# One slot size for the rest of an attention and mixture-of-experts kernel

## The chip, the cores and the metric

The kernel runs on one core of a Trainium2 chip. The metric is the device time of one execution in microseconds (us), the median over runs. The engines are named PE (TensorE), DVE (VectorE), ACT (ScalarE), POOL (GpSimd) and SP (SyncE); PEld is PE's weight load.

## What is computed

First an attention over 8 batches of 8 heads, 576 tokens of 64 values each, that keeps only the scores within `tau` of the row's maximum; then each of the 4608 tokens (512 values) goes through the one of 8 experts that its gate picks:

```python
scores = scale * np.matmul(q, k.transpose(0, 1, 3, 2))
thresh = np.max(scores, axis=-1, keepdims=True) - tau
scores = np.where(scores >= thresh, scores, -1000000000.0)
attn = softmax(scores)
x = concat_heads(np.matmul(attn, v))                  # 4608 x 512
logits = x @ w_gate + modality_bias[modality_id]
e_idx = np.argmax(logits, axis=1)
for e in range(8):
    mask = e_idx == e
    h = np.maximum(x[mask] @ w1[e], 0.0)              # 512 -> 1024
    out[mask] = gate_w[mask, None] * (h @ w2[e])      # 1024 -> 512
```

## The kernel before, in words

The attention goes through 32 pairs of heads, 9 steps to a pair. When a batch is done, its tokens are routed: `route_a` to `route_b` give every token a place, and `scatter` (line 681) writes its number and its gate's weight into a table `tab` in DRAM with indirect DMAs of POOL. The table has one region of CAP rows for each expert, and a row that holds no token holds the number N, which later gathers and scatters skip. The table is filled with N early on, in `late_constants` (lines 256 to 259): POOL sets a tile `fill`, and SP writes it out. `fill` shares the tag `xr` with the tiles in which the attention's output leaves.

While the attention runs, full slots of tokens are already sent through their expert, interleaved with it: SIDE (line 71) lists seven of them, of 256, 384, 512, 512, 512, 448 and 512 rows. `pick` (line 691) chooses the expert for each. What is left at the end, the rest, is planned by `pick_rest` (line 708) on DVE, on one partition: for three slot sizes, 512, 384 and 256 (SIZES), it counts how many slots each expert needs, and gives the expert and the table position of each slot, in `si`. ALWAYS slots of 512 rows (three) are written into the program without a condition; all others lie in a nest of branches at the end (`more`, line 1202), within an outer branch on the number of further slots (lines 1209 to 1214), which each engine loads by `ask` (line 1125). Before the outer branch ACT copies one value of the last output tile into `done_y` (line 1210).

`slot` (line 780) writes one slot. SP loads the expert and the table position into registers (lines 795 and 799), then the table rows `tb` (line 801) and the weights `raw` (lines 838 and 842). POOL gathers the tokens, 128 rows to a tile `xg` (line 814). PE transposes them (line 828); weights and tokens are each split into a high and a low part (lines 303, 304, 856 to 860), and each product takes three matmuls. The first layer is line 874, its ReLU lines 885 and 886. The second layer, line 901, goes over 2 halves of the hidden layer, the row tiles, and 4 chunks in each; ACT (line 909) and DVE (line 914) scale and add the halves, and POOL scatters the tile `y` to the output (line 916).

PE's and POOL's orders are those in which the code is written out, by due times (`at`, `put`); the orders of DVE, ACT and SP are the framework's scheduler's, within chains that `stamp_issue_order_token` fixes. `finish` (line 1112) gives the attention's memory back and opens new pools for the rest, their buffers and the planning's tiles among them; from there the matmuls write into new PSUM banks, `pm`, in place of `bk`.

## Time and profile before

| | |
|---|---|
| runs | 1012.5, 1012.56, 1022.66 us |
| median | 1012.56 us |
| the profiled execution's own time | 1011.88 us |
| its span, first to last instruction | 1010.2 us |
| granted TensorE clock, mean | 0.998 |

The profile is of one execution. A busy time is that of an engine's instructions, without its waits; PE's matmuls overlap, and their ends are modelled. A wait is put down to what ended it. A `q` behind an engine's name is its sequencer, which branches, loads registers and issues DMAs. In the chain of waits, "issue" is time for which the profile shows no wait.

### The profile page before, as it was taken

The numbers are of one execution on the slowest core, as the hardware profiler recorded it, in microseconds if no ns is written. First come the engines' busy times: TensorE is split into PE (matmuls) and PEld (weight loads), VectorE is DVE, ScalarE is ACT, GpSimd is POOL, SyncE is SP. The second block draws the span as 40 slices with busy tenths as digits, with TensorE's granted clock in tenths as the row PEclk, the third lists the DMA queues.
The fourth block names the chain that finished last, engine by engine and source line by source line (L and its number), as shares of the span: only waits on it lengthen the run. The fifth ranks groups of instructions, "written<-read, shape, count | busy, mean of one in ns | idle before, by whom it ended". The sixth has DMA issues, their size and how long they took to land.

```text
span 1010.2 us, 20293 instructions
## 1 busy us (share of the span) xinstructions
PE 986.6 (98%) x6556; PEld 795.0 (79%) x6556; DVE 681.3 (67%) x1698; ACT 633.5 (63%) x1439; POOL 524.8 (52%) x728
## 2 busy tenths in 40 slices
PE   7999999999999999999999999999999999999996
PEld 6777777788888887788778888788878867888885
DVE  6888987778677766777677877777766764333422
ACT  6787887676676666666667666666667625334430
POOL 4363467377538553655455654646567274534311
PEclk9999999999999999999999999999999999999999
DMA  6667777679647665676647555667666227634301
GB/s 154 145 158 169 137 196 196 169 161 237 170 124 168 187 159 133 144 184 163 165 112 177 153 158 133 152 160 197 153 150 165 82 81 200 204 108 139 116 10 44
DMA packets 206803, 151.83 MB, mean 150 GB/s; under 512 B 100062, under 2 KB 167646, under 8 KB 206688
## 3 DMA queue, kind: packets, MB, share of 16 engines
q1 hardware_dynamic: 199488, 131.53, 53.0%
q0 software_dynamic: 7200, 18.92, 5.9%
q8 instruction: 54, 0.88, 0.4%
q14 instruction: 61, 0.50, 0.2%
HBM read 80.05 MB, written 19.48 MB: 99 GB/s over the span
## 4 chain that ended last, share of the span: by engine, by line
PE 74%; DVE 9%; issue 9%; DMA 2%; ACT 2%; POOL 2%; SPq 1%; POOLq 0%; DVEq 0%; ACTq 0%
PE bk L521 15%; PE s L402 14%; PE bk L487 10%; PE bk L901 10%; PE bk L874 10%; PE pm L901 4%; PE pm L874 3%; DVE pr L459 2%; DVE nm L435 2%; PE bk L339 2%; PE bk L828 2%; PE bk L512 1%; PE bk L573 1%; ACT e L445 1%; DMA xg<-xs,tb 1%
## 5 line engine op out<-in xcount | busy, mean ns | idle before, releaser
L435 DVE TENSOR_REDUCE nm<-s 128x1 f32<-128x576 f32 x254 | 190.9, 752 | 97.4 <-PE s L402 95.3
L459 DVE SCALAR_TENSOR_TENSOR pr<-s,nm,e 128x576 f32<-128x576 f32 x254 | 204.8, 815 | 62.7 <-ACT e L445 58.9
L445 ACT ACTIVATE e<-s,nm 128x576 f32<-128x576 f32 x254 | 188.6, 743 | 59.5 <-DVE nm L435 52.6
L402 PE MATMUL s<-km,q 128*128 128x288 f32 x1024 | 196.5, 313 | 7.5 <-DVE pr L459 6.4
L497 ACT COPY ptm<-bk 128x512 f32<-128x512 f32 x256 | 149.4, 584 | 53.2 <-PE bk L487 52.6
L487 PE MATMUL bk<-ident,pr 128*128 128x128 f32 x1152 | 173.8, 273 | 0.0
L402 PEld LDWEIGHTS s<-km,q 128*128 128x128 f32 x1024 | 146.3, 189 | 24.5 <-DVE pr L459 18.2
L487 PEld LDWEIGHTS bk<-ident,pr 128*128 128x128 f32 x1152 | 140.6, 140 | 27.3 <-issue 6.2
L521 PE MATMUL bk<-ptm,v_m 128*64 128x320 f32 (+1 forms) x1024 | 140.7, 412 | 0.3 <-DVE hl L886 0.3
L860 POOL TENSOR_TENSOR w2l<-raw,w2h 128x512 fp32r<-128x512 f32 x77 | 98.5, 1287 | 32.6 <-ACT w2h L856 28.6
L521 PEld LDWEIGHTS bk<-ptm,v_m 128*64 128x64 f32 x1024 | 68.2, 136 | 50.8 <-issue 7.9
L916 POOL DMA_INDIRECT out_dram<-y,tb x37 | 38.0, 1026 | 122.2 <-DVE y L914 92.2
L476 ACT COPY rp<-pr 128x64 f32<-128x64 f32 x271 | 60.0, 248 | 43.8 <-DVE pr L459 41.5
L874 PE MATMUL bk<-xh,w1h 128*128 128x512 f32 (+3 forms) x204 | 82.1, 402 | 0.1
L313 POOL CAST nk<-str 128x64 fp32r<-128x64 f32 x31 | 7.4, 240 | 138.3 <-ACT str L327 130.9
L874 PE MATMUL bk<-xl,w1h 128*128 128x512 f32 (+3 forms) x204 | 74.2, 363 | 0.0
L874 PE MATMUL bk<-xh,w1l 128*128 128x512 f32 (+3 forms) x204 | 74.1, 363 | 0.0
L901 PE MATMUL bk<-w2h,hh 128*128 128x512 f32 x168 | 73.4, 437 | 0.0
L860 POOL TENSOR_TENSOR w1l<-raw,w1h 128x512 fp32r<-128x512 f32 x53 | 68.1, 1285 | 4.2
L901 PE MATMUL bk<-w2h,hl 128*128 128x512 f32 x168 | 66.2, 394 | 0.0
L901 PE MATMUL bk<-w2l,hh 128*128 128x512 f32 x168 | 66.1, 393 | 0.0
L814 POOL DMA_INDIRECT xg<-xs,tb x37 | 39.0, 1053 | 38.4 <-DMA tb<-tab 16.5
(211 smaller groups left out, 1973.6 us busy)
## 6 DMA issues: line engine op xcount, KB each, us to landing
raw<-in_moe_w_dram SPq DMA_DIRECT2D x160, 256.0 KB, 3.5
q<-nq SPq DMA_DIRECT2D x124, 256.0 KB, 4.4
km<-nk SPq DMA_DIRECT2D x124, 144.0 KB, 2.5
v_m<-in_v_dram SPq DMA_DIRECT2D x32, 256.0 KB, 3.7
xs<-xr SPq DMA_DIRECT2D x32, 256.0 KB, 3.0
k_m<-in_k_dram SPq DMA_DIRECT2D x62, 128.0 KB, 3.2
q_m<-in_q_dram SPq DMA_DIRECT2D x62, 128.0 KB, 3.7
vr<-in_v_dram SPq DMA_DIRECT2D x64, 16.0 KB, 4.1
```

The lines of the kernel that those rows point to most:

```text
L402: nc.tensor.matmul(out=sps[:, hf, 0:SH], lhsT=a, rhs=x, start=(z == 0), stop=(z == len(passes) - 1))
L435: in_line(nc.vector.tensor_reduce(out=nm[:, 0:1], in_=sv, axis=AX.XY, op=ALU.max, negate=True), two)
L445: in_line(nc.scalar.activation(out=e, in_=sv, func=AF.Exp, bias=nm[:, 0:1]), two and n < LEAD)
L459: in_line(nc.vector.scalar_tensor_tensor(out=pr.rearrange("p (a x) -> p a x", a=2), in0=s2[n % 2][:, :, 0:SH], scalar=th, in1=e, op0=ALU.i ...
L476: (nc.gpsimd.tensor_copy if 2 <= n < 46 else nc.scalar.copy)(out=state[("rp", p)][:, 2 * c + s + x, :], in_=pr[:, SA:S])
L487: nc.tensor.transpose(out=ps[:, kc * P:(kc + 1) * P], in_=pr[:, kc * P:(kc + 1) * P], identity=ident)
L497: in_line(nc.scalar.copy(out=ptm[:, s, :, (c % 2) * P:(c % 2 + 1) * P], in_=pv), n + 2 < LEAD)
L521: nc.tensor.matmul(out=o, lhsT=lhsT, rhs=rhs, start=start, stop=stop, skip_group_check=True)
L814: nc.gpsimd.indirect_dma_start(out=xg, out_offset=None, in_=xs[0:nrow, :], in_offset=bass.IndirectOffsetOnAxis(ap=box["tb"][:, t, 0:1].bit ...
L860: then(eng.tensor_tensor(out=lo, in0=raw, in1=hi.bitcast(F32), op=ALU.subtract), eng is nc.vector and (lined or late))
L874: nc.tensor.matmul(out=ps[:, 0:WT], lhsT=a[:, cs], rhs=x[:, c, :], start=(c == 0 and z == 0), stop=(c == KC - 1 and z == 2))
L901: nc.tensor.matmul(out=ps, lhsT=h[:, ts], rhs=w, start=(z == 0 and y == 0), stop=(z == F2 - 1 and y == 2))
```

## The change

The rest is planned in slots of 512 rows alone. `pick_rest` has one count per expert in place of three and writes a smaller `si`; MAXC, the most slots that can come, becomes 16. The table's regions are one slot longer (CAP from 4608 to 5120 rows), and the table's fill goes out in two DMAs from a tile of half the size. The gathers, the scaling and the scatters work on the rows of their tile that the slot has (`w = TP(t)`), where they worked on 128. At the end, the nest of branches hangs directly on the number of slots, `done_y` and the outer branch go, and so does the packing of two halves (`pack`), which only slots of 256 rows used.

```diff
@@ -61,21 +61,17 @@
     NT = NC + 1
     SH = S // 2
     W = 512
-    CAP = -(-N // W) * W
-    NCH = CAP // W
+    NCH = -(-N // W)
+    CAP = (NCH + 1) * W
     TROWS = NE * CAP + 2 * W
-    WH = W // 2
     WM = 384
     U = 64
-    SIDE = [(WH, 1), (WM, 2)] + [(W if b != B - 2 else W - U, b) for b in range(3, B)]
-    SIZES = (W, WM, WH)
-    MAXN = ((N - NE * (WM + 1)) // W + NE if N >= NE * (WM + 1) else N // (WM + 1),
-            min(NE, N // (WH + 1)), NE)
-    left_ = max(W, N - sum(w for w, _ in SIDE))
-    ALWAYS = (-(-left_ // W), 0, 0)
-    MAXC = max(MAXN)
+    SIDE = [(W // 2, 1), (WM, 2)] + [(W if b != B - 2 else W - U, b) for b in range(3, B)]
+    WR = W
+    MAXC = (N - NE) // WR + NE
+    ALWAYS = -(-max(W, N - sum(w for w, _ in SIDE)) // W)
     KC = DM // P
     FC = DF // P
     scale = 1.0 / float(D) ** 0.5
...
@@ -186,14 +182,12 @@
     lg = glob.tile([P, NT, H + 1, NE], F32, name="lg")
     nc.gpsimd.memset(lg[:, NC], 0.0)
     taken0 = iota([1, NE], [[CAP // U, NE]], "taken0", base=W // U)
-    th_lo = iota([1, NE, NCH], [[0, NE], [W, NCH]], "th_lo")
+    th_lo = iota([1, NE, NCH], [[0, NE], [WR, NCH]], "th_lo")
     ij = iota([1, MAXC], [[1, MAXC]], "ij")
     tri = glob.tile([1, NE, NE], F32, name="tri")
     nc.gpsimd.memset(tri, 1.0)
     nc.gpsimd.affine_select(out=tri, in_=tri, compare_op=ALU.is_ge, fill=0.0,
                             base=0, pattern=[[1, NE], [-1, NE]], channel_multiplier=0)
-    cnt = glob.tile([1, 4, NE], F32, name="cnt")
-    nc.gpsimd.memset(cnt[:, 0], 0.0)
     pay = glob.tile([P, B, NT, 2], I32, name="pay")
     nc.gpsimd.iota(pay[:, :, 0:NC, 0], pattern=[[S, B], [1, NC]], base=0, channel_multiplier=NC)
     nc.gpsimd.iota(pay[:, :, NC, 0], pattern=[[S, B]], base=SA, channel_multiplier=1)
...
@@ -253,10 +247,12 @@
                                         in1=mid_f[:, m, :].unsqueeze(2).to_broadcast(shp), op=ALU.mult)
             nc.gpsimd.tensor_tensor(out=bias_t, in0=bias_t, in1=bias_u, op=ALU.add)
-        fill = work.tile([P, TROWS // P, 2], I32, name="fill", tag="xr", bufs=2)
+        half = TROWS // P // 2
+        fill = work.tile([P, half, 2], I32, name="fill", tag="xr", bufs=2)
         nc.gpsimd.memset(fill[:, :, 0], N)
         nc.gpsimd.memset(fill[:, :, 1], 0)
-        nc.sync.dma_start(out=tab.rearrange("(p r) c -> p r c", p=P), in_=fill)
+        for y in range(2):
+            nc.sync.dma_start(out=tab[y * half * P:(y + 1) * half * P, :].rearrange("(p r) c -> p r c", p=P), in_=fill)
         return bias
...
@@ -714,60 +710,39 @@
         taken = fin["xp"].tile([1, NE], F32, name="taken", bufs=1)
         nc.vector.tensor_tensor(out=taken, in0=done, in1=taken0, op=ALU.subtract)
-        th = fin["xp"].tile([1, 3, NE, NCH], F32, name="th", bufs=1)
-        for z, w in enumerate((WM, WH, 0)):
-            nc.vector.scalar_tensor_tensor(out=th[:, z], in0=th_lo, scalar=float(w),
-                                           in1=left.unsqueeze(2).to_broadcast([1, NE, NCH]),
-                                           op0=ALU.add, op1=ALU.is_lt)
-        nc.vector.tensor_reduce(out=cnt[:, 1:4, :], in_=th, axis=AX.X, op=ALU.add)
...
+        th = fin["xp"].tile([1, NE, NCH], F32, name="th", bufs=1)
+        nc.vector.tensor_tensor(out=th, in0=th_lo, in1=left.unsqueeze(2).to_broadcast([1, NE, NCH]), op=ALU.is_lt)
+        ns = fin["xp"].tile([1, NE], F32, name="ns", bufs=1)
+        nc.vector.tensor_reduce(out=ns, in_=th, axis=AX.X, op=ALU.add)
+        cum = fin["xp"].tile([1, NE], F32, name="cum", bufs=1)
+        t = fin["xp"].tile([1, NE, NE], F32, name="cum_t", bufs=1)
+        nc.vector.tensor_tensor(out=t, in0=ns.unsqueeze(1).to_broadcast([1, NE, NE]), in1=tri, op=ALU.mult)
+        nc.vector.tensor_reduce(out=cum, in_=t, axis=AX.X, op=ALU.add)
         SHP = [1, MAXC, NE]
...
+        le = fin["xp"].tile(SHP, F32, name="le", bufs=1)
+        nc.vector.tensor_tensor(out=le, in0=ij.unsqueeze(2).to_broadcast(SHP),
+                                in1=cum.unsqueeze(1).to_broadcast(SHP), op=ALU.is_ge)
+        ej = fin["xp"].tile([1, MAXC], F32, name="ej", bufs=1)
         nc.vector.tensor_reduce(out=ej, in_=le, axis=AX.X, op=ALU.add)
...
+        si = glob.tile([1, 2 * MAXC + 1], I32, name="si")
+        nc.vector.tensor_scalar(out=si[:, 0:MAXC], in0=ej, scalar1=float(NE - 1), scalar2=None, op0=ALU.min)
+        off = fin["xp"].tile([1, NE], F32, name="off", bufs=1)
+        nc.vector.tensor_tensor(out=off, in0=cum, in1=ns, op=ALU.subtract)
+        nc.vector.tensor_scalar(out=off, in0=off, scalar1=float(-WR), scalar2=None, op0=ALU.mult)
+        nc.vector.scalar_tensor_tensor(out=off, in0=taken, scalar=float(U), in1=off, op0=ALU.mult, op1=ALU.add)
+        em = fin["xp"].tile([1, MAXC], F32, name="em", bufs=1)
         nc.vector.tensor_scalar(out=em, in0=ej, scalar1=float(-NE), scalar2=None, op0=ALU.add)
...
+        nc.vector.tensor_tensor(out=le, in0=em.unsqueeze(2).to_broadcast(SHP),
+                                in1=iota_m[0:1, :].unsqueeze(1).to_broadcast(SHP), op=ALU.is_equal)
+        nc.vector.tensor_tensor(out=le, in0=le, in1=off.unsqueeze(1).to_broadcast(SHP), op=ALU.mult)
+        bj = fin["xp"].tile([1, MAXC], F32, name="bj", bufs=1)
         nc.vector.tensor_reduce(out=bj, in_=le, axis=AX.X, op=ALU.add)
...
+        nc.vector.scalar_tensor_tensor(out=bj, in0=ij, scalar=float(WR), in1=bj, op0=ALU.mult, op1=ALU.add)
         nc.vector.scalar_tensor_tensor(out=bj, in0=ej, scalar=float(CAP), in1=bj, op0=ALU.mult, op1=ALU.add)
...
+        nc.vector.tensor_scalar(out=si[:, MAXC:2 * MAXC], in0=bj, scalar1=float(W), scalar2=float(W + NE * CAP),
+                                op0=ALU.add, op1=ALU.min)
+        nc.vector.tensor_copy(out=si[:, 2 * MAXC:], in_=cum[:, NE - 1:NE])
         return si
     prev_out = []
...
@@ -811,9 +786,10 @@
                 xg = xt_pool().tile([P, DM], F32, name="xg", bufs=nx[1])
                 box[("xg", t)] = xg
+                w = TP(t)
                 nc.gpsimd.indirect_dma_start(
-                    out=xg, out_offset=None, in_=xs[0:nrow, :],
-                    in_offset=bass.IndirectOffsetOnAxis(ap=box["tb"][:, t, 0:1].bitcast(U32), axis=0),
+                    out=xg[0:w], out_offset=None, in_=xs[0:nrow, :],
+                    in_offset=bass.IndirectOffsetOnAxis(ap=box["tb"][0:w, t, 0:1].bitcast(U32), axis=0),
                     bounds_check=nrow - 1, oob_is_err=False)
             return f
...
@@ -904,18 +878,18 @@
                     return
                 let_go(ps)
                 tb = box["tb"]
+                w = TP(t)
                 if g == 0:
                     y0 = xp.tile([P, DM], F32, name="y0", bufs=W // P)
-                    nc.scalar.activation(out=y0, in_=ps, func=AF.Copy, scale=tb[:, t, 1:2].bitcast(F32))
+                    nc.scalar.activation(out=y0[0:w], in_=ps[0:w], func=AF.Copy, scale=tb[0:w, t, 1:2].bitcast(F32))
                     box[("y0", t)] = y0
                     return
                 y = xp.tile([P, DM], F32, name="y", bufs=2)
-                fin["y"] = y
-                nc.vector.scalar_tensor_tensor(out=y, in0=ps, scalar=tb[:, t, 1:2].bitcast(F32),
-                                               in1=box.pop(("y0", t)), op0=ALU.mult, op1=ALU.add)
+                nc.vector.scalar_tensor_tensor(out=y[0:w], in0=ps[0:w], scalar=tb[0:w, t, 1:2].bitcast(F32),
+                                               in1=box.pop(("y0", t))[0:w], op0=ALU.mult, op1=ALU.add)
                 i = _inst(nc.gpsimd.indirect_dma_start(
-                    out=out, out_offset=bass.IndirectOffsetOnAxis(ap=tb[:, t, 0:1].bitcast(U32), axis=0),
-                    in_=y, in_offset=None, bounds_check=N - 1, oob_is_err=False))
+                    out=out, out_offset=bass.IndirectOffsetOnAxis(ap=tb[0:w, t, 0:1].bitcast(U32), axis=0),
+                    in_=y[0:w], in_offset=None, bounds_check=N - 1, oob_is_err=False))
                 for o in prev_out:
                     tc.declare_no_dep(i, o, reason="every token has a row of its own")
                 prev_out.append(i)
...
@@ -1093,14 +1066,14 @@
                 t = when(e[0]) - e[2] - (1.5 if e[3] in late and e[3][0] == 1 else 0)
             at(t, e[1])
-    def last_slot(j, z):
+    def last_slot(j):
         def where():
             si = fin["si"]
-            return si[0:1, z, j:j + 1], si[0:1, z, MAXC + j:MAXC + j + 1]
-        return slot(where, lambda: group_bank(), N, SIZES[z], lambda: fin["wp"], (8, 4, FC),
+            return si[0:1, j:j + 1], si[0:1, MAXC + j:MAXC + j + 1]
+        return slot(where, lambda: group_bank(), N, WR, lambda: fin["wp"], (8, 4, FC),
                     lambda which, f_: nc.vector if which == 1 else nc.gpsimd, (lambda: fin["xp"], (2, 4)),
-                    lined=z + j == 0, pack=2 * SIZES[z] == W)
+                    lined=j == 0)
     fin = {}
...
@@ -1123,17 +1096,17 @@
     at(XF, finish)
     def ask():
-        fin["more"] = nc.values_load(fin["more_i"][0:1, 0:1], min_val=0, max_val=sum(MAXN))
+        fin["more"] = nc.values_load(fin["si"][0:1, 2 * MAXC:], min_val=0, max_val=MAXC)
     at(F0 + C['ask'], ask)
     t0 = F0
-    for z in range(3):
-        for j in range(ALWAYS[z]):
-            for e in sum(last_slot(j, z), []):
-                t = t0 + e[0] if len(e) == 2 else min(t0 + e[0], F0 + e[2])
-                if z + j == 0 and getattr(e[1], "key", 0) in C['first']:
-                    t = F0 - 8.15 + C['first'].index(e[1].key) / 1000
-                at(t, e[1])
-            t0 += SIZES[z] / 16
+    for j in range(ALWAYS):
+        for e in sum(last_slot(j), []):
+            t = t0 + e[0] if len(e) == 2 else min(t0 + e[0], F0 + e[2])
+            if j == 0 and getattr(e[1], "key", 0) in C['first']:
+                t = F0 - 8.15 + C['first'].index(e[1].key) / 1000
+            at(t, e[1])
+        t0 += W / 16
     def run_events(lo, hi):
         while True:
             ts = [x for x in events if lo <= x < hi]
...
@@ -1199,19 +1172,14 @@
         at(NSTEP + LAG + z / 2, f)
     run_events(0, 10 ** 9)
-    def more(cnt, j, z):
-        if j < MAXN[z]:
+    def more(cnt, j):
+        if j < MAXC:
             with tc.If(cnt > j):
-                for e in sorted(sum(last_slot(j, z), []), key=lambda x: x[0]):
+                for e in sorted(sum(last_slot(j), []), key=lambda x: x[0]):
                     e[1]()
-                more(cnt, j + 1, z)
-    done_y = tiny.tile([1, 1], F32, name="done_y", bufs=1)
-    nc.scalar.copy(out=done_y, in_=fin["y"][0:1, 0:1])
-    with tc.If(fin["more"] > 0):
-        for z in range(3):
-            m = nc.values_load(fin["si"][0:1, z, 2 * MAXC:], min_val=0, max_val=MAXN[z])
-            more(m, ALWAYS[z], z)
+                more(cnt, j + 1)
+    more(fin["more"], ALWAYS)
 # ---- launch: one core; inputs and outputs as the reference has them ----
```

## Rows read from the trace of the kernel before

**Rows 1.** The page's first part: busy us (share), instructions of each engine.

```profile
PE 986.6 (98%) x6556; PEld 795.0 (79%) x6556; DVE 681.3 (67%) x1698; ACT 633.5 (63%) x1439; POOL 524.8 (52%) x728
```

**Rows 2.** PE's waits: waited for, us in total, times, longest.

```profile
PE s L402 <- DVE pr L459: 6.4, 11, 1.5
```

**Rows 3.** Table by stage: stretch, us, busy of each engine, clock, DMA share, GB/s.

```profile
825.00:836.00 11.00, 11.00 (x50) 9.12 (x49) 10.07 (x46) 3.52 (x6) 7.46 (x7) 1.00 0.19 45
...
861.00:1002.00 141.00, 140.87 (x631) 114.94 (x629) 44.67 (x66) 48.47 (x83) 47.00 (x42) 1.00 0.33 103
1002.00:1011.00 9.00, 0.00 (x0) 0.00 (x0) 0.75 (x1) 0.19 (x1) 0.98 (x1) 0.70 0.15 55
```

**Rows 4.** Line 901: count, ns min/median/max, first and last start us, shape.

```profile
L901 PE MATMUL bk<-w2h,hh x168: 387/474/500, 173.9 to 811.3; 128*128 128x512 f32 x168
...
L901 PE MATMUL pm<-w2h,hh x128: 389/392/481, 830.6 to 1001.1; 128*128 128x512 f32 x128
```

**Rows 5.** Lines 1211 and 1213, the closing branch, in the same columns.

```profile
L1211 POOLq EVENT_SEMAPHORE  x6: 17/30/43, 1007.7 to 1008.1; - x6
...
L1211 POOLq COMPARE_BRANCH  x1: 53/53/53, 1005.1 to 1005.1; - x1
...
nothing on L1213; most used: ['L521', 'L402', 'L487', 'L874', 'L901', 'L459', 'L445', 'L339', 'L476', 'L512', 'L828', 'L838', 'L842', 'L435', 'L497', 'L573', 'L609', 'L442', 'L860', 'L313', 'L354', 'L119', 'L348', 'L314', 'L858']
```

**Rows 6.** Timeline of DVE, the planning's first and last: start, us.

```profile
825.20 0.15 DVE L712 SCALAR_TENSOR_TENSOR left<-done,pos 1x8 f32<-1x8 f32 x1
...
835.03 0.17 DVE L758 TENSOR_SCALAR si<-bj 1x30 int32<-1x30 f32 x1
```

**Rows 7.** Waits of SP's queue, 815 to 850 us: total, times, longest.

```profile
SPq L842 <- POOL w1l L860: 9.1, 1, 9.1
...
SPq L1126 <- DVE si L758: 0.2, 1, 0.2
```

**Rows 8.** Chain of waits, 836 to 862 us: start, us, what.

```profile
842.74 0.28 SPq L799
...
843.56 3.81 DMA tb<-tab
...
848.17 4.78 DMA xg<-xs,tb
852.96 0.14 issue
853.09 0.63 PE bk L828 x4
```

**Rows 9.** Lines 257 and 259, the table's fill, in the columns of rows 4.

```profile
L257 POOL MEMSET fill<- x1: 384/384/384, 53.5 to 53.5; 128x296 int32 x1
...
L259 SPq DMA_DIRECT2D tab<-fill x1: 537/537/537, 56.0 to 56.0; - x1
```

**Rows 10.** Line 916, and POOL's timeline from 816 us (idle time in brackets).

```profile
L916 POOL DMA_INDIRECT out_dram<-y,tb x37: 971/1017/1395, 233.5 to 1004.7; - x37
...
816.40 1.01 POOL L916 DMA_INDIRECT out_dram<-y,tb  x1 [0.15 <-issue]
...
825.20 0.63 POOL L858 CAST w1h<-raw 128x512 fp32r<-128x512 f32 x1 [2.12 <-PE bk L874]
```

**Rows 11.** Timeline of the tail, without PE, in the columns of rows 6.

```profile
999.26 0.75 DVE L914 SCALAR_TENSOR_TENSOR y<-pm,tb,y 128x512 f32<-128x512 f32 x1 [2.00 <-PE pm L901]
...
1000.28 0.97 POOL L916 DMA_INDIRECT out_dram<-y,tb  x1 [1.77 <-DVE y L914]
...
1002.19 0.75 DVE L914 SCALAR_TENSOR_TENSOR y<-pm,tb,y 128x512 f32<-128x512 f32 x1 [2.18 <-PEq L1211]
1002.98 0.19 ACT L1210 COPY done_y<-y 1x1 f32<-1x1 f32 x1 [11.36 <-DVE y L914]
1004.69 0.98 POOL L916 DMA_INDIRECT out_dram<-y,tb  x1 [3.44 <-issue]
```

**Rows 12.** Groups of POOL's instructions, 0 to 16 us: busy, mean ns, idle before.

```profile
L313 POOL CAST nk<-str 128x64 fp32r<-128x64 f32 x1 | 0.2, 236 | 6.3 <-ACT str L327 6.3
```

More of the change, by code (lines that the diff above doesn't have):

```diff
@@ L724, in pick_rest @@
-        ns = fin["xp"].tile([1, 3, NE], F32, name="ns", bufs=1)
-        nc.vector.tensor_tensor(out=ns, in0=cnt[:, 1:4, :], in1=cnt[:, 0:3, :], op=ALU.subtract)
-        off = fin["xp"].tile([1, 3, NE], F32, name="off", bufs=1)
-        nc.vector.scalar_tensor_tensor(out=off, in0=taken.unsqueeze(1).to_broadcast([1, 3, NE]),
-                                       scalar=float(U) / W, in1=cnt[:, 0:3, :], op0=ALU.mult, op1=ALU.add)
-        cum = fin["xp"].tile([1, 3, NE], F32, name="cum", bufs=1)
@@ L758, in pick_rest @@
-        nc.vector.tensor_scalar(out=si[:, :, MAXC:2 * MAXC], in0=bj, scalar1=float(W + NE * CAP), scalar2=None,
-                                op0=ALU.min)
-        nc.vector.tensor_copy(out=si[:, :, 2 * MAXC:], in_=cum[:, :, NE - 1:NE])
-        more_f = fin["xp"].tile([1, 3, 1], F32, name="more_f", bufs=1)
-        for z in range(3):
-            nc.vector.tensor_scalar(out=more_f[:, z], in0=cum[:, z, NE - 1:NE], scalar1=float(-ALWAYS[z]), scalar2=0.0,
-                                    op0=ALU.add, op1=ALU.max)
```

36 lines of the change are left out of this document (3 added, 33 removed).

## The prediction

> **What bounds the kernel now.** I read the page's busy shares first: TensorE (PE) is busy 986.6 us of a span of 1010.2 us, the next engine, VectorE (DVE), 681.3 us [rows 1]. So what the change can give is what PE stands idle, and what it can take is a new wait of PE. The table by stage then says where the idle time lies: from 861 to 1002 us, while the rest is worked off, PE is busy 140.87 of 141 us, and after 1002 us it has nothing left to do, while the core still runs for 8.2 us more (1010.2 - 1002) [rows 3]. Before 1002 us PE is idle 1002 - 986.6 = 15.4 us in all. The largest entry of PE's waits is 6.4 us in 11 waits for the masked softmax, spread over the attention [rows 2]; the change does not touch that code. The two ends to look at are therefore the planning of the rest (825 to 853 us) and the tail (after 1002 us).
>
> **How often the rest's slot runs.** This decides whether the change moves 46 us or nothing, so it comes first. The second product's line, 901, has 168 groups of three matmuls into the old banks and 128 into the new ones [rows 4]. A slot of 512 rows has 2 halves x 4 row tiles x 4 chunks = 32 such groups; the side slots of 256 and 384 rows have 16 and 24. 168 = 16 + 24 + 4 x 32, and 128 = 32 (the last side slot) + 96: three slots of 512 rows for the rest, which is ALWAYS[0]. Line 1213, the first line inside the closing branch, left no instruction [rows 5], so the kernel's count of further slots was 0: no slot of 384 or 256 rows, at most three of 512. The new count per expert is the number of thresholds 0, 512, 1024, ... below what is left; the old three counts add up to exactly that. So the new plan also comes to at most three slots, and three always run. The reference's own routing says the same: 476, 497 and 499 rows are left with three experts. The matmuls do not change, and neither does a row of the work of these slots, whose last tiles are full tiles.
>
> **The change, part by part.**
>
> *Planning on DVE.* Lines 712 to 769 run 39 instructions between 825.20 us and 835.03 + 0.17 = 835.20 us, 10.0 us with other DVE work between them [rows 6]. The new text has 20. At the 10.0 / 39 = 0.26 us that an instruction now has of the stretch, 19 fewer are worth 4.9 us of DVE. DVE is full in that stretch (10.07 of 11 us), but PE is too (11.00 of 11 us) [rows 3]: it works on the last side slot, which covers the planning. Who is next in line is SyncE (SP), which loads the plan into registers and issues the rest's loads. SP stood there for 9.1 us waiting for a weight buffer that GpSimd (POOL) releases, and only 0.2 us for the plan's last write [rows 7]. So of 4.9 us at most 0.2 us reach SP. From there the chain is exposed: the register load of the table position at 842.74 us, the table rows, the gather of 4.78 us, and the first transpose at 853.09 us, which PE waited for [rows 8]. I take -0.2 us; 0 if POOL still ends last.
>
> *Tail of the plan.* The copy `done_y` on ScalarE (ACT) goes, and the outer branch goes; the count is compared directly. The branch stays one taken branch over code that isn't run (13 nested slots in place of 23). On POOL, the last engine, the branch is at 1005.1 us and the next instruction at 1007.7 us [rows 5]: 2.6 us, before and after. ACT's copy starts at 1002.98 us, when DVE's last output is ready, and POOL's last scatter, which doesn't read it, starts at 1004.69 us [rows 11]: 0 us, covered by POOL's longer path; if the copy had any part in that scatter's delay, see the rivals.
>
> *Set-up.* A memset of POOL goes and one iota grows from 10 to 16 elements. POOL is idle for 6.3 us before its first cast, waiting for ACT [rows 12]: 0 us. Without that cover it would be some 0.1 us.
>
> *Table fill.* The regions grow from 4608 to 5120 rows, the table from 8 x 4608 + 1024 = 37888 to 41984 rows, 328 per partition; the fill is cut into two DMAs of 164. The two memsets on POOL shrink from 384 ns to 384 x 164 / 296 = 213 ns. SP issues one more DMA, 537 ns [rows 9]. Behind it on SP stand the query copies and the next pair's loads, needed steps later; I take 0 us, and 0.5 us if that cover is gone. The Trainium skill (DMA: Bandwidth & Descriptors, Latency and other measured facts) speaks against this part: it gives each such DMA a first-byte cost of about 0.6 us whatever its size. By it, and were the second DMA exposed, the sum would be 0.6 us larger as an estimate; the row shows only the 537 ns of issue.
>
> *Half-filled last tile.* Only the side slot of 448 rows has one. One gather and one scatter move 64 rows in place of 128, and one ACT and one DVE instruction work on 64 partitions. No row shows an indirect DMA of 64 rows; those of 128 take 1017 ns on POOL [rows 10]. Bounds: 0 us saved, if the time does not hang on the rows, up to 0.5 us each, if it halves. The scatter is the one at 816.40 us; a POOL that is earlier there waits longer at 825.20 us, where it waited for PE [rows 10]. So 0 us.
>
> *Memory.* The planning tiles shrink, so the rest's buffers lie elsewhere in the memory that the attention gives back. No row shows which old tile then lies beneath them. From below 0 us; from above one more DMA round before the rest's first tile, for which the nearest row is the table load, 843.56 to 847.37 us, just ahead of the gather [rows 8]: 3.8 us. I take 0, because the attention's stages are over by then.
>
> Sum: -0.2 us. The profiled execution has a span of 1010.2 us and lasted 1011.88 us, 0.68 us under the median of 1012.56 us. I predict 1012.3 us for the median.
>
> **Rivals.**
>
> *The tail loses its gap.* The scatter before the last starts 0.27 us after DVE ends its tile (999.26 + 0.75 = 1000.01, 1000.28); the last one 1.75 us after (1002.94, 1004.69) [rows 11]. In that time ACT copies `done_y` and the engines load the count. If these are what held POOL, 1.5 us go: 1010.8 us. Against it: POOL waits for none of them.
>
> *The rest starts late* (the other side). One of the rest's first buffers now waits for an old tile. It decides from the first 0.1 us, since PE already waits at 853.09 us: up to 3.8 us as above, 1016.1 us. For it: the memory does move. Against it: most of it has been free for long.
>
> *A second taken branch.* The Trainium skill (Runtime: NRT & Kernel Launch, Instruction fetch mechanics) says that a taken branch out of the fetched pages stalls for a fetch; the trace agrees, by the 2.6 us above. If the nest of 13 left each engine by two branches and not one, that would be 2.6 us: 1014.9 us. The code shows one comparison on the path.
>
> *The order drawn up anew.* The instructions of DVE, ACT and SP are laid out by the framework's scheduler, and one more DMA at 56 us can shift what follows. The price is a wait of PE like the 11 for the softmax, 0.58 us each [rows 2]; 18 more of them give 10 us, 1022.8 us.
>
> *A fourth slot.* 192 matmuls and 16 transposes at 140.87 / 631 = 0.22 us [rows 3]: 46 us, 1058 us. It needs a count that differs from the old one, which the counts above exclude but for an error in the new text.
>
> **How the numbers follow.** Forecast 0.65; tail without gap 0.10; rest late 0.12; second branch 0.03; new order, slower 0.06, faster 0.02; fourth slot 0.02. A measurement of this kernel can tell about 1% from no change, 10 us. Within it lie the first four, 0.90; slower by more: 0.06 + 0.02 = 0.08; faster by more: 0.02, since PE's whole idle time before 1002 us is 15.4 us. The range takes in the tail without gap, less the 0.5 us of each half tile's DMA (1010.8 - 1.0 = 1009.8), and the late rest with the exposed DMA issue (1016.1 + 0.5 = 1016.6): 1009.8 to 1016.6 us.
>
> **What would show it.** Right: 128 groups of line 901 in the new banks, DVE's planning down to 20 instructions and near 5 us, PE idle again for about 0.5 us before the first gathered tile, PE busy 986 to 987 us, and some 8 us after PE's last matmul. Wrong: more matmuls, PE waiting longer than 1 us at the first transposes of the rest, new waits of the score matmuls after 56 us, or a last scatter that follows its tile by 0.3 us.

## The result, and the profile after

The changed kernel takes 1029.07 us (median of 7 runs, 1028.34 to 1034.03). The kernel before, run beside it on the same chip, takes 1015.88 us (7 runs, 1012.5 to 1022.66). The ratio is 1.0135, 95% interval 1.0115 to 1.0155: the change makes the kernel slower by 1.35%, where 1012.3 us against 1012.56 was forecast with a range that ended at 1016.6 us. The runs of before that the prediction started from had a median of 1012.56 us; 1.0135 times that is 1026.2 us.

The profiled execution of the changed kernel lasted 1034.03 us, with a span of 1032.3 us (1010.2 before). The page's first part, with the busy time, share and instructions of each engine, answers to [rows 1]:

```profile
PE 993.8 (96%) x6556; PEld 798.7 (77%) x6556; DVE 676.7 (66%) x1679; ACT 633.6 (61%) x1438; POOL 523.1 (51%) x727
```

PE runs the same 6556 matmuls. The table by stage (stretch, us, busy of each engine, clock, DMA share, GB/s) answers to [rows 3]:

```profile
825.00:836.00 11.00, 9.66 (x58) 7.43 (x58) 8.00 (x30) 2.35 (x6) 8.06 (x12) 1.00 0.37 112
...
861.00:1002.00 141.00, 139.31 (x621) 113.43 (x622) 46.22 (x68) 51.00 (x88) 52.94 (x46) 0.99 0.38 113
1002.00:1014.00 12.00, 12.00 (x52) 9.43 (x51) 2.95 (x4) 0.60 (x1) 2.92 (x3) 1.00 0.14 51
1014.00:1032.00 18.00, 0.04 (x1) 0.00 (x0) 0.75 (x1) 0.00 (x0) 0.97 (x1) 0.57 0.08 27
```

PE ends at 1014.0 us in place of 1002.0, and then the core runs for 18 us with nearly nothing busy, where it ran for 8.2. So the 22.1 us of span fall into two parts: 12 us ahead of PE's end, 10 us behind it.

**Behind PE's end.** What fills the tail is not counted as busy: two instructions of POOL's sequencer, INC_SWDGE_SEM (by its name a semaphore update) and DRAIN. They are seen when one asks for the instructions of POOL on the line of the closing branch and on the program's last line, those of the engine's sequencer included (count, ns min/median/max, first and last start). Of before:

```profile
L1211 POOLq INC_SWDGE_SEM  x1: 348/348/348, 1008.2 to 1008.2; - x1
...
L1241 POOLq DRAIN  x3: 40/107/732, 1008.6 to 1009.9; - x3
```

Of after:

```profile
L1177 POOLq INC_SWDGE_SEM  x1: 2468/2468/2468, 1019.2 to 1019.2; - x1
...
L1209 POOLq DRAIN  x3: 40/107/9389, 1021.7 to 1031.6; - x3
```

The first drain of the three grows from 0.73 to 9.39 us, the semaphore instruction ahead of it from 0.35 to 2.47 us: 8.66 + 2.12 = 10.8 us. In the timeline of after, the last scatter (start, us, operation, idle before and its releaser) starts at

```profile
1015.62 0.97 POOL L890 DMA_INDIRECT out_dram<-y,tb  x1 [2.32 <-DVE y L888]
```

that is 0.28 us after DVE ends its tile, where it stood 1.75 us off before [rows 11]. So the tail gains 1.5 us there and loses 10.8, 9.3 us in sum. The 0.7 us that are left of the 10.0 lie in small differences; 0.3 of them are between PE's end and DVE's last tile.

**Ahead of PE's end.** PE's waits (total, times, longest) answer to [rows 2]; the softmax is as before, the gathered rows are not:

```profile
PE s L398 <- DVE pr L455: 6.4, 11, 1.5
PE bk L804 <- DMA xg<-xs,tb: 5.9, 4, 2.1
```

Two of these four waits are near 2 us, at the first tile of the first side slot and at the first tile of the rest, and behind each the clock drops (columns as in the table by stage):

```profile
143.00:147.00 4.00, 3.81 (x17) 2.00 (x17) 1.62 (x7) 0.60 (x2) 1.47 (x2) 0.50 1.00 219
147.00:151.00 4.00, 4.00 (x27) 4.00 (x26) 1.11 (x2) 2.87 (x8) 2.94 (x6) 0.70 0.02 4
...
857.00:862.00 5.00, 3.45 (x16) 2.52 (x14) 2.24 (x5) 4.30 (x8) 3.03 (x3) 1.00 0.83 213
862.00:867.00 5.00, 4.42 (x17) 3.67 (x18) 1.22 (x2) 0.93 (x2) 4.67 (x5) 0.66 0.63 187
```

After a wait of 2.0 us the granted clock was 0.50 (1.2 of 2.4 GHz) from 143 to 147 us. After the wait of 2.1 us at the rest, with PE busy for 3.45 of the 5 us from 857 us on, it stood at 0.66 on average from 862 to 867 us. Whether the change brings this, or this one execution, the next section says.

### The profile page after: what moved, and what is told of

Its sections match the earlier page's. It is cut to its first block, busy times and chain, and to the rows that moved or that the text cites. A ratio compares the mean times of both kernels' runs of the same rounds, so it can differ in the third digit from the quotient of the medians.

```text
span 1032.3 us, 20269 instructions
## 1 busy us (share of the span) xinstructions
PE 993.8 (96%) x6556; PEld 798.7 (77%) x6556; DVE 676.7 (66%) x1679; ACT 633.6 (61%) x1438; POOL 523.1 (51%) x727
## 3 DMA queue, kind: packets, MB, share of 16 engines
q0 software_dynamic: 7136, 18.92, 5.9%
## 4 chain that ended last, share of the span: by engine, by line
PE 71%; issue 10%; DMA 6%; DVE 5%; POOL 4%; SPq 1%; ACT 1%; POOLq 0%; DVEq 0%; ACTq 0%
PE bk L517 14%; PE s L398 13%; PE bk L875 10%; PE bk L483 10%; PE bk L850 10%; PE pm L875 3%; PE bk L335 2%; PE pm L850 2%; DMA xg<-xs,tb 2%; PE bk L804 1%; DVE pr L455 1%; PE bk L508 1%; DVE nm L431 1%; POOL w2l L836 1%; PE bk L569 1%
## 5 line engine op out<-in xcount | busy, mean ns | idle before, releaser
L309 POOL CAST nk<-str 128x64 fp32r<-128x64 f32 x31 | 7.4, 238 | 141.1 <-ACT str L323 138.6
L836 DVE TENSOR_TENSOR w1l<-raw,w1h 128x512 fp32r<-128x512 f32 x27 | 19.4, 720 | 61.8 <-ACT w1h L832 61.8
```

The lines of the kernel that those rows point to most:

```text
L836: then(eng.tensor_tensor(out=lo, in0=raw, in1=hi.bitcast(F32), op=ALU.subtract), eng is nc.vector and (lined or late))
```

## The experiments

The theory at the start was that the half-filled tile's transfers lengthen POOL's last drain (rows). The rivals were the table with its second fill (table), the missing copy `done_y` (copy), and variation from one execution to the next. The table sums up all runs. The ratio is to runs of before on the same chip; a kernel without a ratio ran once, for its trace. The spans are of one profiled execution each, and chips differ, so spans are compared within a chip alone: e1 to e8 ran on one chip, e9 to e11 on a second, e12 and e13 on a third, e14 to e16 on a fourth.

| kernel | ratio [95%] | INC_SWDGE_SEM, us | longest DRAIN, us | last scatter behind its tile, us | PE's end, us | span, us |
|---|---|---|---|---|---|---|
| before (first profile) | 1 | 0.35 | 0.73 | 1.75 | 1002.0 | 1010.2 |
| after (first profile) | 1.0135 [1.0115, 1.0155] | 2.47 | 9.39 | 0.28 | 1014.0 | 1032.3 |
| e1 after again | 1.0136 [1.0114, 1.0159] | 2.47 | 9.39 | 0.28 | 1006.5 | 1024.4 |
| e2 after, full rows | 1.0050 [1.0031, 1.0068] | 0.35 | 0.73 | 1.75 | 1008.2 | 1017.2 |
| e3 after, old table | 1.0121 [1.0102, 1.0140] | 2.47 | 9.39 | 0.28 | 1005.4 | 1023.2 |
| e4 after, with done_y | 1.0114 [1.0096, 1.0133] | 2.47 | 9.39 | 0.28 | 1005.0 | 1022.9 |
| e5 before, half rows | 1.0102 [1.0083, 1.0121] | 2.47 | 9.39 | 0.28 | 1001.1 | 1018.6 |
| e6 after, gather alone half | 1.0148 [1.0125, 1.0171] | 2.47 | 9.39 | 0.28 | 1006.8 | 1024.6 |
| e7 after, scatter alone half | 1.0153 [1.0128, 1.0178] | 2.47 | 9.39 | 0.28 | 1006.5 | 1024.8 |
| e8 before again | | 0.35 | 0.73 | 1.75 | 1003.2 | 1011.4 |
| e9 planning alone | 1.0026 [1.0008, 1.0044] | 0.35 | 0.73 | 1.75 | 1012.1 | 1021.0 |
| e10 before, 96 rows | | 2.47 | 9.38 | 0.28 | 1010.5 | 1028.5 |
| e11 before, gather as 64 + 64 | | 0.35 | 0.73 | 1.76 | 1009.7 | 1018.4 |
| e12 planning alone, old layout | 1.0008 [0.9992, 1.0025] | 0.35 | 0.73 | 1.75 | 1010.4 | 1019.8 |
| e13 before, 64 + 64 apart | | 0.35 | 0.73 | 1.76 | 1008.3 | 1016.4 |
| e14 after, 128 rows more | 1.0031 [1.0014, 1.0048] | 0.35 | 0.73 | 1.76 | 1008.3 | 1017.3 |
| e15 before, 64 rows more | | 0.35 | 0.73 | 1.76 | 1002.9 | 1011.5 |
| e16 before, 128 rows more | 0.9976 [0.9957, 0.9996] | 0.37 | 0.81 | 0.28 | 1004.1 | 1011.8 |

### Which part costs (e1 to e4)

**e1, after again.** No edit; a second trace. 

> The changed kernel once more, for a second trace of it. In its first trace two stretches were longer than before the change: PE reached the first product of the first side slot 6.0 us late, of the second 8.1 us late, and after PE's last matmul the core ran on for 18.2 us in place of 8.2, of which POOL's last drain took 9.39 us (0.73 before). If both belong to the change, both come again: PE's end at 1012 to 1015 us and a tail of 14 us or more. If either was an accident of that one execution, it is gone here, while the time against before stays at 1.013.

The two long instructions of the tail came out as in the first trace, to the nanosecond. PE's end did not: 1006.5 in place of 1014.0 us. Two waits for a gather stand in its list in place of four, and the clock held:

```profile
PE bk L804 <- DMA xg<-xs,tb: 2.2, 2, 1.5
...
143.00:147.00 4.00, 4.00 (x35) 3.16 (x34) 2.85 (x10) 3.30 (x12) 3.31 (x7) 1.00 0.89 215
```

So 7.5 of the 12 us ahead of PE's end belong to the first recorded execution and its chip (beside it before, too, took up to 1022.66 us), not to the change. Traces of the kernel before with small edits, on the chip of e9 to e11, show the same: the first transpose of the first side slot started at 144.4 us in e11 and 145.7 us in e10, against 140.1 us in the first trace of before, 142.2 us in e8, and 143.2 us in the first trace of after.

One of the two waits of e1 stays, though: that at the rest's first tile, 1.5 us long, where before waits 0.5 us. The lines are those of before from 840 us on and of e1 from 800 to 870 us; the section on the rest of the loss comes back to them.

```profile
PE bk L828 <- DMA xg<-xs,tb: 0.5, 1, 0.5
```

```profile
PE bk L804 <- DMA xg<-xs,tb: 1.5, 1, 1.5
```

**e2, full rows.**

```diff
-                w = TP(t)
+                w = P
```

(in the gather and in the scatter) 

> The changed kernel, with gathers, scaling and scatters of 128 rows in the half-filled last tile again. Theory rows: the transfers of 64 rows leave POOL's queue in a state that the last drain pays for; then the drain is back under 1 us, the tail at about 8 us, and the ratio to before at 1.003 to 1.006. Theories table and tail: no difference to the changed kernel, 1.012 to 1.015, with a drain of several us.

The ratio falls from 1.0136 to 1.0050 on the same chip and the drain to 0.73 us:

```profile
L1177 POOLq INC_SWDGE_SEM  x1: 348/348/348, 1014.9 to 1014.9; - x1
...
L1209 POOLq DRAIN  x3: 40/107/732, 1015.3 to 1016.6; - x3
```

The transfers of 64 rows cost 0.86%, 8.7 us. The theory (rows) stands so far; 0.5% is left to explain.

**e3, old table.**

```diff
-    CAP = (NCH + 1) * W
+    CAP = NCH * W
-        half = TROWS // P // 2
...
-        for y in range(2):
...
+        nc.sync.dma_start(out=tab.rearrange("(p r) c -> p r c", p=P), in_=fill)
```

> The changed kernel, with regions of 4608 rows and the fill as one DMA again. Theory table: the longer regions or the second fill DMA make the table's and the token rows' transfers land late, and PE waits at the first gathers; then the first product of the first side slot comes within 1 us of its time before (145.0 us) and the ratio falls by 0.006 to 0.008, to about 1.006. Theories rows and tail: the wait at the first gathers stays, the ratio stays at 1.012 to 1.015.

1.0121 against 1.0136, with intervals that overlap; the tail is unchanged. By these ratios the table is worth 0.15%, about 1.5 us, and it may be nothing. The traces point the same way: on this chip the first side slot's first transpose comes at 141.1 to 142.2 us in the three kernels with the old table (e3, e5, e8) and at 142.3 to 143.4 us in the five with the new one (e1, e2, e4, e6, e7); on the chip of e14 to e16 it comes at 143.3 us with the new table and at 141.5 and 142.1 us with the old one. That is some 1.3 us, from few traces, and whether the longer regions or the second transfer would do it was not tested apart.

**e4, the copy.**

```diff
+                fin["y"] = y
...
+    done_y = tiny.tile([1, 1], F32, name="done_y", bufs=1)
+    nc.scalar.copy(out=done_y, in_=fin["y"][0:1, 0:1])
```

> The changed kernel, with ACT's copy of the last output tile ahead of the branch again. Theory tail: without the copy ACT takes its branch 12 us early, and the end of the program pays for it; then the last drain is back under 1 us, the tail at 8 to 10 us and the ratio at 1.003 to 1.006. Theories rows and table: no difference, 1.012 to 1.015.

The tail is unchanged: the copy neither made the gap ahead of the last scatter nor shortens the drain. 1.0114 lies 0.2% under e1, again within the intervals. In the trace e4 needs 473.6 us from the first transpose of the third side slot to that of the seventh and last one, where e1, e2 and e3 need 474.4 us. That 0.8 us is not the copy's: the kernel before takes 473.6 us in e8 and 474.5 us in its first trace, with no edit between them.

### What makes the drain long (e5 to e7, e10, e11, e13 to e16)

**e5, the half rows alone, in the kernel before.**

```diff
-                    out=xg, out_offset=None, in_=xs[0:nrow, :],
+                    out=xg[0:w], out_offset=None, in_=xs[0:nrow, :],
...
-                    in_=y, in_offset=None, bounds_check=N - 1, oob_is_err=False))
+                    in_=y[0:w], in_offset=None, bounds_check=N - 1, oob_is_err=False))
```

> The kernel before with one part of the change alone: the gather, the scaling and the scatter of a half-filled last tile take 64 rows. Theory rows (transfers of 64 rows make the end of the program long): ratio 1.007 to 1.010, POOL's last DRAIN 9.4 us in place of 0.73, INC_SWDGE_SEM 2.5 us in place of 0.35, some 18 us after PE's last matmul. Rival together (the half rows cost this only with the new tail, without the outer branch and the copy done_y): ratio within 0.998 to 1.002, DRAIN 0.7 us.

This part alone makes the old kernel slower by 1.02%, and with the old tail, `done_y` and outer branch included, it has the long drain:

```profile
L1213 POOLq INC_SWDGE_SEM  x1: 2468/2468/2468, 1005.9 to 1005.9; - x1
...
L1243 POOLq DRAIN  x3: 40/107/9389, 1008.4 to 1018.3; - x3
```

Its PE ended earlier than in either trace of before (1001.1 us): nothing is lost ahead of the tail.

**e6 and e7, one half transfer alone** (in the changed kernel, `w = P` in the scatter only, then in the gather only). 

> The changed kernel with a scatter of 128 rows again; only the gather of the half-filled tile takes 64 rows. If the gather makes the drain long: DRAIN 9.4 us, ratio about 1.013. If the scatter does: DRAIN 0.73 us, ratio about 1.005.

> The changed kernel with a gather of 128 rows again; only the scaling and the scatter of the half-filled tile take 64 rows. If the scatter makes the drain long: DRAIN 9.4 us, ratio about 1.013. If the gather does: 0.73 us, ratio about 1.005. If both count: DRAIN about 5 us here and in the other half.

Either one of them gives the whole drain, 9.39 us. So it doesn't go by how many half transfers there are, one or two.

**e8, before again**, for the variation of its trace. 

> The kernel before a second time, for its trace. If the first gathers' lateness in the changed kernel (2 to 6 us at the first transposes of the first side slot) is the variation of DMA landings from run to run: this trace too has its first transposes some us away from the 140.1 us of the first trace. If it comes of the change: 140 us within 0.5 us, and the span 1009 to 1011 us.

The first transpose came at 142.2 us, 2.1 us off the first trace, and the span was 1011.4 us. The lateness at the first gathers varies by that much with no edit at all.

**e10, 96 rows.**

```diff
+                w = P if TP(t) == P else 96
```

> The kernel before, with 96 rows in place of 128 in the gather, the scaling and the scatter of the half-filled last tile (64 of them are the slot's own). If any transfer of fewer than 128 rows costs the long drain: DRAIN 9.4 us, INC_SWDGE_SEM 2.5 us, span 1018 to 1021 us. If the drain goes by the rows that are missing: about half of the rise, DRAIN 5 us. If only 64 rows do it: DRAIN 0.73 us, span 1010 to 1012 us.

The long drain again, 9.38 us: nor does it go by how many rows are missing.

**e11, the gather as two of 64.**

```diff
+                for r0, r1 in (((0, P),) if TP(t) == P else ((0, P // 2), (P // 2, P))):
+                    nc.gpsimd.indirect_dma_start(
+                        out=xg[r0:r1], out_offset=None, in_=xs[0:nrow, :],
...
```

> The kernel before; the gather of the half-filled last tile is issued as two transfers of 64 rows each, one right behind the other, 128 rows in sum (the second one repeats the first one's rows into rows that nothing reads); the scatter has 128 rows. If the drain goes by the sum of rows that POOL has written at the end: DRAIN 0.73 us, span 1010 to 1012 us. If one transfer of 64 rows anywhere is enough: DRAIN 9.4 us, INC_SWDGE_SEM 2.5 us, span 1018 to 1021 us.

Two transfers of 64 rows give the short drain:

```profile
L1242 POOLq DRAIN  x3: 40/107/732, 1016.8 to 1018.1; - x3
```

This refutes the theory in its first form: a transfer of fewer than 128 rows is not what costs.

**e13, the second half later.**

```diff
+                if TP(t) < P:
+                    w = TP(t)
+                    again = xt_pool().tile([P, DM], F32, name="xg", bufs=nx[1])
+                    nc.gpsimd.indirect_dma_start(
+                        out=again[0:w], out_offset=None, in_=xs[0:nrow, :],
...
```

(behind the scatter; the gather itself with 64 rows) 

> The kernel before; the gather of the half-filled last tile takes 64 rows, and a second gather of the same 64 rows, into a tile that nothing reads, is issued right behind the full scatter of that tile, with other transfers between the two. If the long drain goes by the sum of the rows in one direction: DRAIN 0.73 us, span near that of the kernel before. If full transfers between the two half ones are enough for it: DRAIN 9.4 us, INC_SWDGE_SEM 2.5 us, the span 8 to 9 us longer.

The short drain, with full transfers between the two. In all these traces one column of the table goes with the drain: where the drain is long, the last scatter follows its tile by 0.28 us, and where it is short by 1.75 us. So there is a step of POOL of some 1.5 us ahead of one transfer; where it comes ahead of the last one, the end is short. Two readings were left: the total of rows decides where the step falls (before, e11 and e13 issue as many, the long ones 64 or 128 fewer), or gathers and scatters must each add up to full transfers.

**e14, the changed kernel with one more gather of 128 rows** (the edit of e13 with 128 in place of `w`). 

> The changed kernel, half transfers and all, with one more gather of 128 rows, which nothing reads, right behind the scatter of the half-filled tile. POOL issues as many rows in all as in the kernel before: 64 + 64 + 128. If the total of rows decides: DRAIN 0.73 us, INC_SWDGE_SEM 0.35 us, last scatter 1.75 us behind its tile, ratio 1.003 to 1.007. If gathers and scatters must each add up to full transfers: DRAIN 9.39 us, 2.47 us, 0.28 us, ratio 1.012 to 1.016.

64 + 64 + 128 rows: as many as before in all, though each direction is 64 off. The drain is short, the scatter 1.76 us behind its tile, the ratio 1.0031:

```profile
L1183 POOLq INC_SWDGE_SEM  x1: 348/348/348, 1014.8 to 1014.8; - x1
...
L1215 POOLq DRAIN  x3: 107/182/732, 1015.2 to 1016.8; - x3
```

With more work the changed kernel loses 0.31% to before, and without it 1.35%. Of the two readings the total is left. The total is one of rows issued, and not of the data that moves: the profile page's line of POOL's queue (packets, MB, share) has the same 18.92 MB in before and in after, in fewer packets (packets and rows fall together here).

```profile
q0 software_dynamic: 7200, 18.92, 5.9%
```

```profile
q0 software_dynamic: 7136, 18.92, 5.9%
```

**e15 and e16, the kernel before with 64 and with 128 rows more** (the same edit). 

> The kernel before with one more gather of 64 rows, which nothing reads, behind the scatter of the half-filled tile: 64 rows more in all. If the total decides, and the step ahead of the last scatter comes at a certain total: DRAIN near 0.73 us (or somewhat more), and the step of 1.5 us ahead of the last scatter moves to an earlier place or stays. If any sum that is not made of full transfers costs the long drain: DRAIN 9.39 us, scatter 0.28 us behind its tile.

> The kernel before with one more gather of 128 rows, which nothing reads: all transfers full, 128 rows more in all. If fullness decides: DRAIN 0.73 us and the last scatter 1.75 us behind its tile, as before. If the total decides: DRAIN other than with 64 more, or again 0.73 us with the step of 1.5 us ahead of the last but one scatter, where it is hidden, and then the time up to 1.5 us shorter (ratio 0.998 to 1.000).

With 64 more, all stays as before: drain 0.73 us, 1.76 us. With 128 more the step moves forward by one scatter: the last but one starts 1.75 us behind its tile (1003.9 us), where PE still works, and the last one 0.28 us.

```profile
L1217 POOLq INC_SWDGE_SEM  x1: 368/368/368, 1009.7 to 1009.7; - x1
...
L1247 POOLq DRAIN  x3: 40/107/814, 1010.1 to 1011.5; - x3
```

So the step comes ahead of the first transfer that starts with enough rows issued, and the two instructions at the end get longer with what POOL issued since: one transfer, 348 and 732 ns; two, 368 and 814 ns. At 20 and 82 ns for each more, the 2468 and 9389 ns of the changed kernel are worth (2468 - 348) / 20 = 106 and (9389 - 732) / 82 = 106 transfers more, so about 107 of the program's 114: nearly all of them, no step having come near the end. That is an estimate, on a line through two points; that both instructions give the same count speaks for it. Why it is not all 114 stays open: no trace shows an earlier step, as no other indirect transfer of any run starts behind an unexplained idle time ("issue") of more than 1.1 us. The Trainium skill (DMA: Bandwidth & Descriptors, SWDGE vs HWDGE vs iDMA) says that GpSimd writes the descriptors of such transfers into rings in SBUF. A step that comes after so many rows would fit the end of such a ring; no run here shows the ring itself, so this is argued, not shown. The place of the step is bounded by the runs: in before it comes with 113 x 128 = 14464 rows issued, and it doesn't come ahead of the last transfer in e6, e7 and e10, with 64 fewer, 14400. These counts hold the 40 scatters of the table, the 37 gathers and the 37 scatters of the output.

e16 is also the one kernel here whose ratio lies under 1, by 0.24% (0.9976, interval 0.9957 to 0.9996), some 2.4 us. The mechanism can give at most the 1.5 us, less the 0.1 us by which the end is longer. In its one trace the tail is 1011.8 - 1004.1 = 7.6 us, where before and e8 have 8.2: 0.6 us, as DVE's last tile starts 0.9 us behind PE's end there and 0.2 us in before. The measured 2.4 us are more than that, but the interval reaches down to 0.4 us; one interval of some dozen that misses 1 by so little may also be chance.

### The rest of the loss (e9, e12)

**e9, the planning alone** (full rows, the old table and the copy put into the changed kernel, as in e2, e3 and e4). 

> The changed kernel with three of its parts undone: transfers of 128 rows for the half-filled tile, the old length of the table regions with one fill transfer, and the copy done_y before the closing branch. What is left is the planning in one slot size and the branch without its outer level. If the 0.5% that the changed kernel with full rows still loses comes of the table and of the layout in memory: ratio within 0.999 to 1.002, PE's last matmul at 1001 to 1004 us, DRAIN 0.73 us. If it comes of the planning: ratio 1.003 to 1.005, the rest's first transpose over 52.5 us behind the first transpose of the last side slot.

1.0026, so of e2's 0.50% about half may have gone with the table and the copy (the intervals overlap and the chips differ: which of the two, or neither, is not settled), and half is left. PE's groups in the rest (mean ns of one) show a part of it. Of the first trace of before, then of e9:

```profile
L901 PE MATMUL pm<-w2h,hh 128*128 128x512 f32 x112 | 45.0, 402 | 0.0
...
L901 PE MATMUL pm<-w2h,hl 128*128 128x512 f32 x112 | 43.7, 390 | 0.0
```

```profile
L873 PE MATMUL pm<-w2h,hh 128*128 128x512 f32 x112 | 45.2, 404 | 0.0
L873 PE MATMUL pm<-w2h,hl 128*128 128x512 f32 x112 | 44.2, 395 | 0.0
```

The matmuls of `w2h` with `hl` take 395 in place of 390 ns (from start to start 235 in place of 230 ns), and from the rest's first transpose to PE's end 149.9 us in place of 148.9 (853.09 to 1001.97). PE waits for nothing more there; it is slower by 0.7%. The other kernels with the new planning in its new shapes, after, e1 to e4, e6, e7 and e14, show it too (149.9 us; 151.5 us in the first trace of after, with its clock), and none without it (148.8 to 148.9 us).

**e12, the planning tiles in their old shapes.**

```diff
-        th = fin["xp"].tile([1, NE, NCH], F32, name="th", bufs=1)
+        th = fin["xp"].tile([1, 3, NE, NCH], F32, name="th", bufs=1)[:, 0]
...
-        le = fin["xp"].tile(SHP, F32, name="le", bufs=1)
+        le = fin["xp"].tile([1, 3 * MB, NE], F32, name="le", bufs=1)[:, 0:MAXC]
...
```

> The kernel of e9 (new planning, full rows, old table, done_y) with the planning tiles allocated in their old shapes (and the four that went allocated again, each written once, three instructions of DVE more), so that the memory behind them is laid out as before. If the slower matmuls of the rest come of the layout: w2h with hl at 230 ns in the rest (235 now), first transpose of the rest to PE's last matmul 148.8 us (149.9 now), ratio 1.000 to 1.002. If they come of something else in the planning part: 235 ns and 149.9 us again, ratio 1.002 to 1.004.

```profile
L878 PE MATMUL pm<-w2h,hh 128*128 128x512 f32 x112 | 45.0, 402 | 0.0
...
L878 PE MATMUL pm<-w2h,hl 128*128 128x512 f32 x111 | 43.3, 390 | 0.0
```

390 ns again, 148.9 us from the rest's first transpose to PE's end. So this 1.0 us, 0.1%, comes not of the new planning's instructions but of the shapes of its tiles, and so of where the tiles behind them come to lie. Which address does it is open. The ratio of 1.0008 is not told from 1, but not from e9's 1.0026 either: the intervals overlap, and the chips differ.

**The rest's start.** One more cost stands in the traces, though no run was made for it. In the ten kernels with the new planning SP loads the rest's first table rows 18.8 to 19.4 us after its last write of the attention's output, in the eight with the old one 17.7 to 18.8 us. PE then waits 0.3 to 2.1 us at the rest's first tile in the former, 0 to 0.5 us in the latter. From the last side slot's first transpose to the rest's first transpose 52.1 to 53.9 us pass with the new planning, 52.8 on average, and 51.6 to 52.3 us with the old one, 51.9 on average. So the rest starts some 0.9 us later on average with the new planning, though the two ranges meet (e9, with 52.1 us, lies within that of the old one). What delays SP is open.

## Why the prediction was wrong, step by step

**The step that failed is *Half-filled last tile*, "So 0 us".** It bounded the part from the side of a gain alone, 0 to 0.5 us for each transfer, by the duration of the issuing instruction on POOL. That term was right: the scatter of 64 rows is the shortest of all, where the one of before took 1.01 us [rows 10] (line 890 in the columns of [rows 4], and POOL's timeline):

```profile
L890 POOL DMA_INDIRECT out_dram<-y,tb x37: 948/1021/1397, 241.0 to 1015.6; - x37
...
824.32 0.95 POOL L890 DMA_INDIRECT out_dram<-y,tb  x1 [0.15 <-issue]
```

What it left out is that the length of POOL's last instructions goes by all the rows that POOL has issued. The trace of before showed the place, though not as a busy time: the 0.35 and 0.73 us of those two instructions, and the 1.75 us ahead of the last scatter. The measured term is 8.66 + 2.12 - 1.5 = 9.3 us, by itself 1.0102 in e5. "Below nothing too" was never asked of this part, though no row showed a transfer of 64 rows; with an unknown operation the bound of the loss belongs beside that of the gain. No rival held the mechanism. The 0.08 for slower by more than 10 us came from two rivals that did not happen: for *the order drawn up anew*, PE's waits for the softmax are 6.4 us in 11 waits as before; for *a fourth slot*, see below.

***Tail of the plan* and the rival *The tail loses its gap*.** The copy costs nothing, as forecast. The gap did go, by the 1.5 us forecast for this rival, and the sign named ("a last scatter that follows its tile by 0.3 us") appeared. But its cause was another: e2, without the copy, has the gap, and e5, with it, hasn't. The row read as "issue", a wait that nothing explained, was the step of POOL that at the old total of rows fell there. The tail of "some 8 us" became 18.

**Memory.** The layout moved, and that cost; but not through a wait, for which 0 to 3.8 us were bounded. PE's matmuls in the rest got slower by 1.0 us together (e9, e12). The size was within the bounds by luck: the mechanism was not among them.

**Planning on DVE.** The step was right in its count and its length: 20 instructions, all but one from 833.04 us to 838.58 + 0.16 = 838.74 us, 5.7 us with other work between them (5 forecast). The one, `taken`, comes ahead of the stretch (822.53 us), as in before (814.60 us, so that 38 and not 39 lie in the 10.0 us). Timeline of after, the first and the last:

```profile
833.04 0.15 DVE L708 SCALAR_TENSOR_TENSOR left<-done,pos 1x8 f32<-1x8 f32 x1
...
838.58 0.16 DVE L743 TENSOR_SCALAR si<-bj 1x16 int32<-1x16 f32 x1
```

The gain of 0.2 us did not show. SP's path went past POOL's `w1l` as the prediction said it could, now with 3.1 us of wait for the plan and then 5.8 for `w1l`, 8.9 in sum, where it was 0.2 and 9.1 [rows 7]:

```profile
SPq L818 <- POOL w1l L836: 5.8, 1, 5.8
SPq L1099 <- DVE off L732: 3.1, 1, 3.1
```

SP's next weight load came 9.5 us after its last write of the attention's output (9.3 in before). But from there to the table rows it took longer, and the rest started some 0.9 us later on average (the section on the rest of the loss): a cost where a gain of 0.2 us was forecast.

***How often the rest's slot runs*** was right: PE's count of matmuls is unchanged and the new banks have 128 groups. In the columns of [rows 4]:

```profile
L875 PE MATMUL pm<-w2h,hh x128: 388/393/774, 838.5 to 1013.2; 128*128 128x512 f32 x128
```

**Set-up and *Table fill*** were right within what the ratios tell: e3's is 0.15% under e1's with intervals that overlap, so neither the 0 nor the 0.5 us is refuted. The first side slots that come some 1.3 us later with the new table (e3) speak for a cost above both. The page's estimate of 0.6 us (the Trainium skill, DMA: Bandwidth & Descriptors, Latency and other measured facts) is not tested by that either.

**The rivals** *a second taken branch* and *a fourth slot* did not come. POOL's branch of after stands at 1016.0 us and its next instruction at 1018.8 us: 2.8 us, one stall as before (2.6) [rows 5]. *The rest starts late* came in part: PE waited 2.1 us at the rest's first tile in the first trace of after, 1.5 in e1 and 1.2 in e2, above the 1 us that was named as a sign of being wrong, but 0.3 us in e9. Its reason, an old tile beneath one of the rest's buffers, is not borne out: e12, with the old layout, waits 0.6 us too.

**Sums.** 1012.56 - 0.2 is 1012.36, which the prediction has as 1012.3 us, and 18 waits of 0.58 us are 10.4 us, so that the new order would have come to 1022.7 and not 1022.8 us; nothing hangs on either.

In sum, of 1.35%: the half rows 1.0% (e5; 0.86% by e1 and e2), the layout behind the planning tiles 0.1% (e9, e12), the rest's later start some 0.1% (seen in the traces, cause open), the table perhaps 0.1% (e3, not shown). What is left is no more than the ratios' intervals.

## What to carry to other kernels

A part that issues less can still cost at the program's end: here POOL's last two instructions went from 1.1 to 11.9 us by 64 or 128 rows fewer in the whole program. Look at the sequencer's instructions of the last lines too, which no busy share counts, and see what they depend on. Where a profile shows an operation's cost in one shape only, bound a new shape on both sides. An unexplained idle time ("issue") ahead of a single instruction, out of many alike, may be a step of that engine that an edit can move, as here to an earlier place (e16) or out of the program's end (e5). A second trace of the same kernel belongs to every difference of 1 or 2 us, and one trace in which an effect is smaller does not show that it is gone.

## What the runs showed of the hardware

- After its indirect transfers POOL's INC_SWDGE_SEM and DRAIN at the program's end took 0.35 and 0.73 us with one transfer since the last step of 1.5 us, 0.37 and 0.81 us with two, 2.47 and 9.39 us where no step came near the end. The total of rows issued decides: 64 or 128 fewer than in before (e5 to e7, e10) give the long end, as many or 64 or 128 more (e11, e13 to e16) the short one. Transfers of fewer than 128 rows do not lengthen it by themselves (e11, e13, e14).
- A scatter of 64 rows kept POOL for 0.95 us, where one of 128 rows in its place took 1.01 us.
- The same matmul of 512 columns took 395 or 390 ns by the shapes of small tiles that lie ahead of its operands in memory (e9, e12): 1.0 us over 149.
- After PE had stood for 2.0 us at the first gather, the granted clock was 0.50 from 143 to 147 us in the first trace of after; in e1, where PE was busy for all of these 4 us, it was 1.00.
